# Input scale folded into C, whole-matrix DMA transposes, an idle Pool and searched ranks in a gated S5 and Hedgehog kernel

## The chip, the cores and the metric

The kernel runs on one core of one Trainium2 chip. The metric is the device time of one execution in microseconds (us).

The engines are named as in the profile: PE does matmuls, PEld is PE's loading of weights (it overlaps with matmuls), DVE is the vector engine, ACT the scalar (activation) engine, POOL the GpSimd engine, SP the engine whose queue issues most DMAs. "PEclk" or "granted clock" is the share of full speed at which PE was allowed to run.

## The reference, cut to what matters

The kernel mixes two sequence layers by a gate (S5, a state space layer, and Hedgehog, a linear attention), for S = 2048 positions of D = 512 channels in bf16.

```python
x = A_x
g = _sigmoid((x * gate_w).sum(-1, keepdims=True))

# A: state space part, P = 512 complex states
dt = jnp.exp(log_dt)
Lam_bar = jnp.exp(dt * Lam)
B_bar = ((Lam_bar - 1.0) / Lam)[:, None] * Bmat      # the "input scale" times B
Bu = jnp.einsum("bld,pd->blp", x + 0j, B_bar)
for t in range(L):
    h = Lam_bar[None, :] * h + Bu[:, t, :]
y = 2.0 * jnp.einsum("blp,dp->bld", hseq, Cmat).real + x * Dskip[None, None, :]

# B: linear attention, 32 heads of 16
pq = einsum(q, w_phi); pk = einsum(k, w_phi)
phi_q = concat([softmax(pq), softmax(-pq)]); phi_k = concat([softmax(pk), softmax(-pk)])
kv = einsum(phi_k, v); z = phi_k.sum(s)
o = (phi_q @ kv) / (phi_q @ z + 1e-6)
b = o @ wo

return g * y + (1 - g) * b
```

One identity carries the change. The recurrence is diagonal in the states and linear in its input. So the factor `(Lam_bar - 1) / Lam`, one complex number per state, may be taken out of B and put on the columns of C instead; the states are then unscaled, and y is the same.

## The kernel before: the parts that matter here

**A planner fixes the order.** The kernel does not issue its instructions in the order of its text. Each piece of work is a task: the engines that may do it with an assumed duration in ns for each, what it depends on, the buffers it takes, and a rank (the highest goes first). A list scheduler inside the kernel places the tasks one by one on a model of the engines. What it assumes is therefore built into the order, but nothing of it slows or speeds an instruction.

```python
for t in reversed(self.tasks):
    t.tail = min(t.eng.values()) + min(LAT[e] for e in t.eng) + max([s.tail for s in t.succ], default=0.0)
    t.key = (-t.rank, -t.tail // QUANT, t.n)
while True:
    ...
    t0 = max(f, min(w[0] for w in rs))
    r, took, t = min((w for w in rs if w[0] <= t0 + WINDOW), key=lambda w: w[2].key)
    ...
self.order = sorted(out, key=lambda t: (t.start, t.n))
```

**B is scaled and transposed on PE.** The scale is computed from the parameters by some 17 tiny DVE operations, spread into twelve 128x128 diagonals, and applied by 64 matmuls that transpose B at the same time. Eight evictions from PSUM (the memory into which matmuls accumulate) then write `BT`.

```python
for kk, v in enumerate((b2r, nb2i, nb2r)):                                    # L529
    VS(out=dgB[:, j, kk, :], in0=ident[:], scalar1=v[:, j:j + 1], scalar2=None, op0=ALU.mult)
...
MM(out=f32v(b)[:, cs], lhsT=Bn[:, 0, j, ds_], rhs=dgB[:, j, c0, :], start=True, stop=False)   # L622
MM(out=f32v(b)[:, cs], lhsT=Bn[:, 1, j, ds_], rhs=dgB[:, j, c1, :], start=False, stop=True)
t = pl.add(_pe(8, 128), mm, deps=t_db + [d_b], bufs=[b, early[3]])
t_bt[ri, dt] = evac_task(BT[:, dt, :, :, ri], b, ...)
```

**Pool builds the recurrence diagonals.** `dgL` holds the complex multiplication by `Lam_bar` as a 128x128 matrix for each of eight blocks of states.

```python
nc.gpsimd.tensor_tensor(out=dgL[:], in0=ident..., in1=lr_[:, 4:12]..., op=ALU.mult)    # L549
nc.gpsimd.tensor_tensor(out=dgS[:], in0=swap..., in1=ns1[:, 4:12]..., op=ALU.mult)     # L553
nc.gpsimd.tensor_tensor(out=dgL[:], in0=dgL[:], in1=dgS[:], op=ALU.add)                # L557
```

**The state space matmuls.** Positions are taken as 512 chunks of four. Positions 0 to 2 of all chunks are kept as partial states `Gs`; the fourth position feeds a scan over the chunks on DVE (`scan_unit`), and `fill_unit` adds the scanned state back to the first three.

```python
MM(out=f32v(b), lhsT=BT[:, kt, tt].rearrange("p q r -> p (q r)"), rhs=xT[...], ...)    # L639
MM(out=f32v(b), lhsT=dgL[:, tt, :], rhs=Gs[:, tt, f - 1, :], start=False, stop=True)   # L644
# fourth position: L653 with BT, L658 with half of dgL
```

**The keys' softmax, and Pool once more.** For each of eight pairs of position tiles, `E` is the exponential, and DVE adds it up in a tree to `st1`. Pool adds `st1` into `smax` (only used for a final range flag). ACT then takes the logarithm in place, so it must wait until Pool has read `st1`.

```python
nc.gpsimd.tensor_tensor(out=smax[:], in0=smax[:], in1=b1.t[:]..., op=ALU.add)          # L773
aact(out=b1.t[:], in_=b1.t[:], func=ACT.Ln)               # deps: prev + t_sx[-1:]
aact(out=rc.t[:], in_=b1.t[:], func=ACT.Exp, scale=-1.0)
VT(out=e5(), in0=e5(), in1=rc.t[:]..., op=ALU.mult)       # normalise E, L777
```

**The join.** After the last pair, the key-value sums leave PSUM as `KVbd` and `SM`. Everything of the queries after this needs them. This code is the same before and after.

```python
VT(out=KVbd[qr, sgn].rearrange("p g (d h) -> p g h d", d=Dh)[:, :, half * 4:half * 4 + 4, :],   # L826
   in0=a4[:, :, :, 0:Dh], in1=mask4[pr]..., op=ALU.mult)
VT(out=SM[qr, sgn, :, 1, half * 4:half * 4 + 4], in0=a4[:, :, :, Dh], in1=mask4[pr]..., op=ALU.mult)   # L828
```

## Time and profile before

| what | before |
|---|---|
| time, median (range) | 182.97 us (182.79 to 183.77, 3 runs) |
| span of the profiled run | 182.4 us |
| PE / DVE / ACT / POOL busy | 162.7 / 146.9 / 108.9 / 18.5 us |
| mean granted clock | 0.950 |
| first state space matmul (L639) | 37.8 us after the start |

The page gives the busy time of each engine, the granted clock in 40 slices of the span (in tenths, 9 is 90% or more), and the share of each engine in the chain of work that ended last. Of the page of the kernel before:

```profile
PE 162.7 (89%) x1274; PEld 89.0 (49%) x1293; DVE 146.9 (81%) x369; ACT 108.9 (60%) x217; POOL 18.5 (10%) x27
...
PEclk9999996999999999999966998589999999999998
...
DVE 47%; PE 36%; DMA 5%; issue 4%; ACT 2%; POOL 2%; SPq 1%; DVEq 0%; POOLq 0%; ACTq 0%
```

PE is the busiest engine at 89%, yet the chain runs over DVE more than over PE. The clock dips in three places: in the slice from 27 to 32 us (the first 6), from 91 to 100 us (66) and from 109 to 123 us (858). The table of stretches shows these places; its columns are the stretch, its length, busy time and number of instructions of PE, PEld, DVE, ACT and POOL, the granted clock, the DMA share and GB/s. Of the kernel before:

```profile
core 0: us, PE busy (x) PEld busy (x) DVE busy (x) ACT busy (x) POOL busy (x), PEclk, DMA share, GB/s
...
25.00:30.00 5.00, 2.64 (x24) 2.28 (x24) 4.89 (x18) 4.35 (x8) 0.00 (x0) 0.75 0.46 105
30.00:35.00 5.00, 4.40 (x57) 3.68 (x56) 4.88 (x9) 4.83 (x7) 0.00 (x0) 0.91 0.43 99
...
90.00:95.00 5.00, 3.62 (x83) 2.75 (x85) 5.00 (x8) 3.44 (x8) 0.00 (x0) 0.74 0.01 3
95.00:100.00 5.00, 5.00 (x15) 1.90 (x14) 4.49 (x14) 3.51 (x8) 0.77 (x1) 0.58 0.20 48
...
110.00:115.00 5.00, 2.54 (x72) 2.07 (x71) 4.92 (x9) 0.77 (x2) 0.00 (x0) 0.78 0.01 3
115.00:120.00 5.00, 4.77 (x46) 2.56 (x45) 4.97 (x16) 1.38 (x5) 0.00 (x0) 0.53 0.00 0
```

In all three places PE pauses while DVE is full or nearly so, and the granted clock falls in the pause and in the stretch behind it. From 115 to 120 us PE is busy for 4.77 us, but at 0.53 of full speed.

Why the first state space matmul comes so late can be read in the timeline. Its columns are the start, the duration, the engine, the line, the operation with its tiles, and in brackets the idle time before it and what ended that. First Pool, then DVE in the same stretch, then PE, all of the kernel before:

```profile
15.38 1.92 POOL L549 TENSOR_TENSOR dgL<-ident,sp 128x1024 bf16<-128x1024 bf16 x1 [4.52 <-DVE sp L508]
20.07 1.92 POOL L553 TENSOR_TENSOR dgS<-swap,sp 128x1024 bf16<-128x1024 bf16 x1 [2.76 <-DVE sp L537]
22.06 2.13 POOL L557 TENSOR_TENSOR dgL<-dgL,dgS 128x1024 bf16<-128x1024 bf16 x1
```

```profile
15.38 0.16 DVE L511 TENSOR_TENSOR sp<-v_66 128x12 f32<-128x12 f32 x1
15.58 1.75 DVE L512 TENSOR_TENSOR sp<-sp 128x12 f32<-128x12 f32 x1
17.25 0.16 DVE L513 TENSOR_SCALAR sp<-sp 128x12 f32<-128x12 f32 x1
...
20.14 1.87 DVE L542 TENSOR_TENSOR sp<-sp 128x12 f32<-128x12 f32 x1
...
22.25 1.98 DVE L545 TENSOR_SCALAR sp<-sp,sg 128x12 f32<-128x12 f32 x1
```

```profile
36.05 1.89 PE L434 MATMUL pp<-Wv,xT 128*128 128x512 bf16 x7
37.78 1.46 PE L639 MATMUL pp<-xT,BT 128*128 128x512 bf16 x6
```

Operations on 128x12 elements take 0.16 us, and three of them take 1.75, 1.87 and 1.98 us. Each of the three begins just after a Pool operation begins and ends with it (15.58 + 1.75 = 17.33 against 15.38 + 1.92 = 17.30). The Trainium skill, "SBUF — State Buffer", section "SBUF: two separate sides", says that GpSimd shares a pair of ports, under an exclusive lock, with DVE operations in a two-port mode or with two SBUF inputs: whoever starts first holds it for its whole instruction and the other blocks fully. This trace agrees, with 1.75 to 1.98 us in place of 0.16. The block is about 5 us of DVE time, on the way to everything that depends on the parameters.

The waits view lists, for an engine and line, what it waited for: total us, number of times, longest. Of the kernel before:

```profile
PE pp L605 <- ACT vx L393: 3.4, 1, 3.4
...
ACT st_1150 L248 <- POOL smax L773: 2.9, 1, 2.9
...
PE pp L907 <- DVE SM L828: 2.4, 1, 2.4
...
ACT st_795 L248 <- POOL smax L773: 2.2, 1, 2.2
```

The logarithm of the keys' softmax waits for Pool's `smax` for 9.3 us in six places together (two are shown). The longest of these waits stands before the second dip of the clock: Pool's addition, 0.45 us at its quickest, takes 1.98 us from 86.84 us on, ACT waits for it, DVE's normalisation of `E` (89.88 us) waits 1.4 us for ACT, and PE waits 1.3 us for that `E` until 91.16 us. PE waits for `SM` at the join, before the third dip.

### The profile page before, as it was taken

The numbers are of one execution on the slowest core, as the hardware profiler recorded it, in microseconds if no ns is written. First come the engines' busy times: TensorE is split into PE (matmuls) and PEld (weight loads), VectorE is DVE, ScalarE is ACT, GpSimd is POOL, SyncE is SP. The second block draws the span as 40 slices with busy tenths as digits, with TensorE's granted clock in tenths as the row PEclk, the third lists the DMA queues.
The fourth block names the chain that finished last, engine by engine and source line by source line (L and its number), as shares of the span: only waits on it lengthen the run. The fifth ranks groups of instructions, "written<-read, shape, count | busy, mean of one in ns | idle before, by whom it ended". The sixth has DMA issues, their size and how long they took to land.

```text
span 182.4 us, 3458 instructions
## 1 busy us (share of the span) xinstructions
PE 162.7 (89%) x1274; PEld 89.0 (49%) x1293; DVE 146.9 (81%) x369; ACT 108.9 (60%) x217; POOL 18.5 (10%) x27
## 2 busy tenths in 40 slices
PE   7699929899999998998799994989999999999980
PEld 2465408744444543452363553655565655566530
DVE  4499999955899997999698999999999992574130
ACT  2288639920773965675567990269998745367200
POOL 6134530000002003101401000000000000000000
PEclk9999996999999999999966998589999999999998
DMA  6999454650004003103102200000101000100111
GB/s 202 295 350 141 117 142 91 146 142 0 0 0 103 15 0 84 33 4 74 41 4 58 58 0 0 4 4 2 59 31 61 29 29 32 59 29 32 45 49 36
DMA packets 17983, 11.85 MB, mean 65 GB/s; under 512 B 10280, under 2 KB 17448, under 8 KB 17960
## 3 DMA queue, kind: packets, MB, share of 16 engines
q1 hardware_dynamic: 17392, 11.54, 23.3%
q8 instruction: 12, 0.20, 0.4%
q10 hardware_dynamic: 568, 0.02, 0.2%
q14 instruction: 11, 0.09, 0.2%
HBM read 4.22 MB, written 2.10 MB: 35 GB/s over the span
## 4 chain that ended last, share of the span: by engine, by line
DVE 47%; PE 36%; DMA 5%; issue 4%; ACT 2%; POOL 2%; SPq 1%; DVEq 0%; POOLq 0%; ACTq 0%
PE pp L961 11%; PE pp L639 6%; PE pp L977 5%; DVE c L692 4%; DVE late L953 3%; DMA xn<-in_A_x_dram 3%; DVE KVbd L826 3%; DVE E L777 3%; DVE c L722 2%; DVE c L723 2%; POOL smax L773 2%; PE pp L753 2%; PE pp L653 2%; PE pp L907 2%; DVE late L955 2%
## 5 line engine op out<-in xcount | busy, mean ns | idle before, releaser
L639 PE MATMUL pp<-xT,BT 128*128 128x512 bf16 x95 | 23.4, 379 | 0.1
L961 PE MATMUL pp<-CT,Gs 128*128 128x512 bf16 x91 | 22.9, 379 | 0.3
L248 ACT ACTIVATE ET<-pp 128x512 bf16<-128x512 f32 x32 | 17.1, 648 | 3.2 <-PE pp L842 3.2
L949 ACT CAST late<-pp 128x512 bf16<-128x512 f32 x32 | 17.0, 615 | 3.0 <-PE pp L946 3.0
L842 PE MATMUL pp<-xT,Wq_70 128*128 128x512 bf16 x61 | 17.2, 431 | 0.7 <-ACT late L949 0.4
L248 ACT ACTIVATE E<-pp 128x512 bf16<-128x512 f32 x32 | 16.3, 613 | 0.9 <-PE pp L753 0.4
L985 DVE TENSOR_SCALAR late<-pp,Gg 128x512 bf16<-128x512 f32 x8 | 6.0, 752 | 12.9 <-PE pp L977 12.9
L977 PE MATMUL pp<-Wo,late 128*128 128x512 bf16 x62 | 16.0, 379 | 0.2 <-issue 0.2
L434 PE MATMUL pp<-Wv,xT 128*128 128x512 bf16 x61 | 14.7, 379 | 0.6 <-ACT xT L393 0.3
L953 DVE TENSOR_TENSOR late<-late 128x512 bf16<-128x512 bf16 x32 | 12.8, 428 | 2.6 <-ACT late L949 2.3
L753 PE MATMUL pp<-Wk_71,xT 128*128 128x512 bf16 x61 | 14.7, 379 | 0.2
L639 PEld LDWEIGHTS <-BT 128*128 128x128 bf16 x96 | 9.3, 98 | 11.1
L961 PEld LDWEIGHTS <-Gs 128*128 128x128 bf16 x96 | 8.9, 98 | 8.8
L393 ACT CAST Gs<-pp 128x512 bf16<-128x512 f32 x17 | 9.9, 604 | 5.2 <-PE pp L644 5.1
L777 DVE TENSOR_TENSOR E<-E,rc 128x2048 bf16<-128x2048 bf16 x8 | 9.8, 1220 | 3.5 <-ACT rc L248 3.5
L973 ACT COPY late<-pp 128x512 bf16<-128x512 bf16 x16 | 9.3, 599 | 5.2 <-PE pp L977 3.6
L842 PEld LDWEIGHTS <-Wq_70 128*128 128x128 bf16 x64 | 6.7, 109 | 9.0 <-issue 4.3
L946 PE MATMUL pp<-KVbd,ET 128*128 128x128 bf16 x128 | 9.6, 219 | 0.1
L393 ACT CAST vx<-pp 128x512 bf16<-128x512 f32 x16 | 8.7, 600 | 1.5 <-PE pp L434 1.2
L961 PE MATMUL pp<-CT,Zs 128*128 128x512 bf16 x31 | 9.3, 439 | 0.2 <-issue 0.2
L434 PEld LDWEIGHTS <-xT 128*128 128x128 bf16 x64 | 6.0, 98 | 6.9 <-issue 0.8
L692 DVE TENSOR_TENSOR_SCAN c<-sp,c 128x512 bf16<-128x512 f32 x8 | 9.3, 1207 | 0.0
(250 smaller groups left out, 314.9 us busy)
## 6 DMA issues: line engine op xcount, KB each, us to landing
xn<-in_A_x_dram SPq DMA_DIRECT2D x4, 512.0 KB, 4.3
Zs<-c SPq DMA_DIRECT2D x32, 64.0 KB, 2.0
out_dram<-late SPq DMA_DIRECT2D x16, 128.0 KB, 1.9
CT<-Gs SPq DMA_DIRECT2D x4, 256.0 KB, 3.4
Wv<-in_B_wqkv_dram SPq DMA_DIRECT2D x1, 512.0 KB, 4.3
Bn<-in_A_B_re_dram SPq DMA_DIRECT2D x1, 512.0 KB
Bn<-in_A_B_im_dram SPq DMA_DIRECT2D x1, 512.0 KB
Wo<-in_B_wo_dram SPq DMA_DIRECT2D x4, 128.0 KB, 2.6
```

Of the source, the lines that this page charges most:

```text
L248: return nc.scalar.activation(**kw)
L393: nc.scalar.copy(out=o, in_=view(b))
L434: MM(out=f32v(b), lhsT=xT[:, kt, tcols(f, a)], rhs=Wv[:, kt, :], start=(kt == 0), stop=(kt == KT - 1))
L639: MM(out=f32v(b), lhsT=BT[:, kt, tt].rearrange("p q r -> p (q r)"), rhs=xT[:, kt, f * NCH:(f + 1) * NCH], start=(kt == 0), stop=(kt == KT ...
L692: nc.vector.tensor_tensor_scan(out=bw_.t[:, ri], data0=rb, data1=b1.t[:, ri], initial=0.0, op0=ALU.mult, op1=ALU.add)
L753: MM(out=f32v(b), lhsT=xT[:, kt, tcols(f, a)], rhs=Wk2[:, kt, :], start=(kt == 0), stop=(kt == KT - 1))
L777: x = pl.add(_dve(1024), lambda e: VT(out=e5(), in0=e5(), in1=rc.t[:].to_broadcast([P, 32, Dh, 4]), op=ALU.mult), deps=[x], bufs=[eb, rc], ...
L842: MM(out=f32v(b), lhsT=Wq2[:, kt, g * P:(g + 1) * P], rhs=xT[:, kt, f * NCH:(f + 1) * NCH], start=(kt == 0), stop=(kt == KT - 1))
L949: tn = pl.add(_act(512), lambda e, sgn=sgn: nc.scalar.copy(out=o2.t[:, sgn], in_=f32v(pn[sgn])), deps=[t], bufs=[pn[sgn], o2], rank=rank + 2)
L953: VT(out=v, in0=v, in1=als[f].t[:, a, sgn * H:(sgn + 1) * H].rearrange("p (g h) -> p g h", g=HG).unsqueeze(2).to_broadcast([P, HG, Dh, 8]) ...
L961: MM(out=f32v(py), lhsT=st, rhs=CT[:, tt, :], start=(tt == 0), stop=False)
L977: MM(out=f32v(py), lhsT=oT.t[:, g, :], rhs=Wo[:, g, :], start=False, stop=(g == HG - 1))
```

## The change

Its intent: B no longer depends on the parameters, so the state space matmuls can begin as soon as a DMA has transposed B; Pool does nothing in SBUF beside DVE's work on the parameters and the softmax; and the order is better fitted. The core of the diff, long cuts marked:

```diff
+UNIT_RANKS = (
+    -3.39, 2.47, -0.13, 1.09, -2.01, 6.16, 9.56, 18.87, 1.24, ...          # 81 shifts
+def shift(self, by):
+    for t in self.tasks:
+        t.rank += by[t.u] if t.u < len(by) else 0.0
 ...
-    nc.sync.dma_start(out=Bn[:, 0], in_=A_B_re.rearrange("(j p) d -> p j d", p=P))
-    nc.sync.dma_start(out=Bn[:, 1], in_=A_B_im.rearrange("(j p) d -> p j d", p=P))
-    for W_, c0 in ((WkT, D), (WqT, 0)):
-        for j in range(KT):
-            nc.sync.dma_start_transpose(out=W_[:, j, :], in_=B_wqkv[:, c0 + j * P:c0 + (j + 1) * P])
+    for ri, B_ in enumerate((A_B_re, A_B_im)):
+        nc.sync.dma_start_transpose(out=BT[:, :, ri, :], in_=B_)
+    nc.sync.dma_start_transpose(out=WkT, in_=B_wqkv[:, D:2 * D])
+    nc.sync.dma_start_transpose(out=WqT, in_=B_wqkv[:, 0:D])
 ...
-    def b_prep():                         # 64 matmuls against dgB, 8 evictions to BT: all gone
 ...
+    # C: two whole-matrix transposes into cb, then the scale: 8 ACT and 8 DVE operations of 128x512
+    nc.scalar.mul(out=tC[:, ri, :], in_=cb.t[:, 1 - ri, j, :], mul=nb2i[:, j:j + 1])
+    nc.vector.scalar_tensor_tensor(out=o, in0=o, scalar=c0[:, j:j + 1], in1=tC[:, ri, :], op0=ALU.mult, op1=ALU.add)
 ...
-    x1 = pl.add({"POOL": 2400.0}, dl1, ...)          # dgL, dgS, their sum, and Dd on Pool
+    pl.add({"ACT": 210.0, "DVE": 165.0}, scaled(dgL[:, tt, :], ident[:], lr_[:, ucol(tt)]), ...)
+    pl.add({"ACT": 210.0, "DVE": 165.0}, scaled(dgS[:, tt, :], swap[:], ns1[:, ucol(tt)]), ...)
+    # sums by DVE; dgX: copies of dgL spread so that the fourth position's matmuls are full width
 ...
-        MM(out=f32v(b), lhsT=BT[:, kt, tt].rearrange("p q r -> p (q r)"), ...)
+        MM(out=f32v(b), lhsT=BT[:, kt].rearrange("p r (q t) -> p (r q) t", t=NT)[:, :, j + 4 * h], ...)
-        MM(out=f32v(b)[h * 64:h * 64 + 64, :], lhsT=dgL[:, 2 * j + h]..., ...)
+        MM(out=f32v(b), lhsT=dgX[:, j, h, ri, :], ...)
 ...
-        nc.gpsimd.tensor_tensor(out=smax[:], in0=smax[:], in1=b1.t[:]..., op=ALU.add)
-        aact(out=b1.t[:], in_=b1.t[:], func=ACT.Ln)      # deps=prev + t_sx[-1:]
+        nc.vector.tensor_reduce(out=smax[:, pair:pair + 1], in_=b1.t[:]..., axis=AX.X, op=ALU.max)   # rank=-3
+        aact(out=lnk.t[:], in_=b1.t[:], func=ACT.Ln)     # deps=prev
 ...
-            cost.update(_dve(256 if bf else 512))
+            cost.update({"DVE": 375.0 if bf else 640.0})
+    pl.shift(UNIT_RANKS)
```

The weights that a state space matmul reads from `BT` are now every eighth element of a row (every fourth at the fourth position), because B arrives transposed as a whole and is not regrouped on the way.

## The prediction

> **What bounds it now.** PE is busy 162.7 of 182.4 us, DVE 146.9, ACT 108.9 (page). From start-to-start times in the timeline (128x512 matmuls 215 ns, 128x128 56 ns) all matmuls need an estimated 149 us at full clock. First transpose 5.0 us, end 5.4 us after PE's last matmul: the floor of this program is about 159 us, so some 23 us are stalls, in three places.
>
> 1. Before the first state-space matmul at 37.8 us (timeline). PE idles 3.4 us before the Wk fold and runs at clock 0.75 and 0.91 in 25-35 us (windows). The chain of waits is DVE: parameters, tables, dgB, eight 0.7 us BT evictions, with b_prep (64 matmuls, 3.6 us) between. Three tiny 128x12 DVE operations take 1.75-1.98 us instead of 0.17, each ending with a Pool operation on dgL or dgS (15.4-17.3, 20.1-22.0, 22.1-24.2 us). The Trainium skill, "SBUF — State Buffer" (shared port pair), says either engine can block the other for a whole instruction; the coinciding ends agree.
> 2. 40-113 us: DVE nearly full, chain DVE/PE. In-place Ln waits for Pool's smax: ACT waits 9.3 us on it in total (waits view); Pool's 0.45 us operation stretches to 1.7-2.0 us twice, on the chain.
> 3. 85-120 us: PE pauses, clock 0.53-0.78. After 150 us the chain is PE.
>
> **Change.** Removed: 64 b_prep matmuls (-3.6 us PE), eight BT evictions (5.8 us, mostly DVE), twelve dgB scalings (2.1 us), Pool's dgL/dgS/Dd/smax with about 5 us of DVE blocking and the smax waits. Added: DVE/ACT take dgL, dgS, Dd, dgX (about 28 operations, 0.17-0.4 us, estimate 6 us), C scaling (8 DVE operations of about 0.7 us, 8 on ACT of 0.6 us), eight max reductions (2.2 us). DVE about -4 us net. The last g3 matmuls become full width: in before, 16 half-width ones cost about 2.5 us because pairs overlap; now 16 x 0.215, +1 us PE. BT weight loads become strided by 8; stride-2 ones took 98 ns like contiguous ones, so I expect no cost.
> Moved: B now gates PE only through its DMA. A 128-column transpose costs 1.26-2.4 us of SP queue; with two B matrices after x, I expect B at about 21 us, Wk at 27, Wq at 32. x transposes and V (18 us PE) fill until then. The first state-space matmul moves from 37.8 to about 22-24 us.
>
> **Sum.** Floor 159 - 3.6 + 1 = 156.5 us. Stalls: stage 1 gives about 9 us, of which some comes back as DVE waits in the middle (DVE still needs some 140 us); middle and joints give 1-3 us; tail unchanged. Net expected -11.5 us: **171.5 us, 80% range 165.5 to 177.5.** Chances: faster 0.95, same 0.04, slower 0.01.
>
> **Would show it right:** timeline: first state-space matmul at 20-26 us; PE clock 1.0 through 20-40 us; no microsecond-long 128x16 DVE operations; Pool idle after about 4 us; no ACT wait on smax; BT weight loads 98 ns; PE total 159-161 us; PE full after about 145 us; chain in the middle still mixed DVE/PE.
>
> **What would make it wrong:** whole-matrix transposes slower on the queue than four chunks, B or Wk landing after 30 us; parameters (now behind x and weights in the SP queue) delaying dgL and tables, so PE starves on recurrences; ACT overloaded before 40 us by scalings plus table loads; offline order fitted to wrong durations (its plan puts 128x512 fills at 268 ns, the trace has 363), so engines stall; C late.

## The result, and the profile after

| what | before | after |
|---|---|---|
| time, median (range) | 183.02 us (182.79 to 183.77, 4 runs) | 168.44 us (168.17 to 169.15, 4 runs) |
| ratio, 95% interval | | 0.9203 (0.9164 to 0.9242): faster |
| span of the profiled run | 182.4 us | 166.7 us |
| PE / DVE / ACT / POOL busy | 162.7 / 146.9 / 108.9 / 18.5 us | 154.2 / 141.8 / 118.0 / 4.6 us |
| mean granted clock | 0.950 | 0.979 |
| first state space matmul | 37.8 us | 21.9 us |

A ratio is the mean time of one kernel's fast runs over the mean of the other's in the same rounds, so it is not quite the ratio of the medians that stand beside it. Where I give a difference between two kernels that were each timed against the kernel before, I subtract their ratios and multiply by 183.0 us; with the intervals found, such a difference is good to about 1 us. The three groups of runs were on different chips (9, 7 and 2 in the record), each beside the kernel before, so this also takes the ratios to be the same on each chip.

Of the page of the kernel after:

```profile
PE 154.2 (92%) x1231; PEld 89.2 (54%) x1231; DVE 141.8 (85%) x377; ACT 118.0 (71%) x240; POOL 4.6 (3%) x12
...
PEclk9999999999999999999999879999999999999995
...
PE 47%; DVE 34%; ACT 7%; DMA 6%; issue 1%; ACTq 1%; SPq 0%; DVEq 0%
```

The dips of the clock at 27 to 32 us and at 91 to 100 us are gone (the 8 and the 7 that are left in the middle, at 92 to 100 us, belong to the join), and the chain now runs over PE first. The same stretches, and those of the join, which now comes at 88 to 93 us, in the kernel after:

```profile
25.00:30.00 5.00, 4.43 (x21) 2.42 (x20) 4.79 (x22) 5.00 (x11) 0.00 (x0) 1.00 1.00 198
30.00:35.00 5.00, 5.00 (x36) 3.29 (x35) 4.41 (x9) 4.97 (x9) 0.00 (x0) 1.00 0.00 0
...
90.00:95.00 5.00, 2.22 (x38) 1.55 (x39) 4.92 (x12) 1.78 (x6) 0.00 (x0) 0.98 0.22 73
95.00:100.00 5.00, 5.00 (x48) 2.44 (x46) 4.97 (x16) 3.91 (x10) 0.00 (x0) 0.68 0.01 2
```

The early stall is gone. The pause at the join is still there, with the low clock behind it. In the timeline of the kernel after, PE reaches the state space matmuls straight from the values (L448) and the gate (L903), and the tiny DVE operations on the parameters take 0.17 and 0.23 us (L525 is one that Pool blocks again in two experiments below, where it stands on L526). First PE, then DVE:

```profile
17.68 2.75 PE L448 MATMUL pp<-Wv,xT 128*128 128x512 bf16 x12
20.27 1.74 PE L903 MATMUL pp<-gw_b,xT 128*128 128x1 bf16 x64
21.87 3.44 PE L679 MATMUL pp<-xT,BT 128*128 128x512 bf16 x15
```

```profile
20.82 0.17 DVE L525 TENSOR_TENSOR sp<-sp 128x16 f32<-128x16 f32 x1
20.90 0.23 DVE L526 TENSOR_SCALAR sp<-sp,sg 128x16 f32<-128x16 f32 x1
```

In the waits view no operation waits for Pool's `smax` any more. Pool still meets DVE once, at the very start: while it clears `dgX` and `KVbd` until 4.96 us, three copies of 64x64 and 128x64 elements by DVE take 1.27 to 1.40 us, and DVE's first eviction starts at 5.93 us instead of 5.66. The wait for `SM` at the join has not shrunk: it was 2.4 us and is now

```profile
PE pp L954 <- DVE SM L872: 3.1, 2, 2.3
```

The span fell by 15.7 us. By the page, 8.5 us of that is PE busy time and the other 7.2 us is PE idle time. The busy time fell by far more than the removed matmuls. They were 64 of 56 ns from start to start, so 3.6 us, and the full-width matmuls of the fourth position took 1.6 us back (4.1 against 2.5 us busy in the groups view). The rest is mostly the clock: 162.7 us at 0.950 lose an estimated 8.1 us to the clock, 154.2 us at 0.979 lose 3.2 us. That is 4.9 + 3.6 - 1.6 = 6.9 of the 8.5 us. The profiled execution of the kernel before was a slow one within its fast state, 184.15 us at 0.950, where its other runs show 0.948 to 0.970, so the spans differ by more than the medians (14.6 us) and the clock's share is at the high end.

### The profile page after: what moved, and what is told of

It is laid out like the page before. It is cut to its first block, busy times and chain, and to the rows that moved or that the text cites. A ratio compares the mean times of both kernels' runs of the same rounds, so it can differ in the third digit from the quotient of the medians.

```text
span 166.7 us, 3342 instructions
## 1 busy us (share of the span) xinstructions
PE 154.2 (92%) x1231; PEld 89.2 (54%) x1231; DVE 141.8 (85%) x377; ACT 118.0 (71%) x240; POOL 4.6 (3%) x12
## 4 chain that ended last, share of the span: by engine, by line
PE 47%; DVE 34%; ACT 7%; DMA 6%; issue 1%; ACTq 1%; SPq 0%; DVEq 0%
PE pp L1009 17%; PE pp L1025 8%; PE pp L887 5%; DVE c L733 4%; PE pp L994 4%; DVE E L821 4%; DMA vq<-in_A_Lambda_im_dram 4%; DVE ET L607 3%; DVE KVbd L870 3%; PE pp L679 3%; PE pp L1012 2%; ACT E L267 2%; DMA vec_n<-in_gate_w_dram 2%; PE pp L1019 2%; PE pp L954 2%; DVE c L737 1%
## 5 line engine op out<-in xcount | busy, mean ns | idle before, releaser
L1009 PE MATMUL pp<-CT,Gs 128*128 128x512 bf16 x96 | 23.8, 379 | 0.1
L267 ACT ACTIVATE E<-pp 128x512 bf16<-128x512 f32 x32 | 16.6, 632 | 2.3 <-PE pp L828 1.6
L679 PEld LDWEIGHTS <-BT 128*128 128x128 bf16 x96 | 13.6, 145 | 8.0 <-issue 1.4
L887 PE MATMUL pp<-xT,Wq_71 128*128 128x512 bf16 x64 | 16.2, 402 | 0.0
L448 PE MATMUL pp<-Wv,xT 128*128 128x512 bf16 x64 | 14.8, 379 | 0.0
L405 ACT CAST Gs<-pp 128x512 bf16<-128x512 f32 x22 | 12.4, 592 | 1.1 <-PE pp L684 0.6
L405 ACT CAST vx<-pp 128x512 bf16<-128x512 f32 x16 | 9.3, 592 | 2.4 <-PE pp L448 2.2
L797 PEld LDWEIGHTS <-xT 128*128 128x128 bf16 x64 | 6.2, 98 | 7.4 <-issue 0.3
L887 PEld LDWEIGHTS <-Wq_71 128*128 128x128 bf16 x64 | 6.1, 101 | 6.8 <-issue 1.1
L448 PEld LDWEIGHTS <-xT 128*128 128x128 bf16 x64 | 6.1, 98 | 6.6
```

The lines of the kernel that those rows point to most:

```text
L267: return nc.scalar.activation(**kw)
L405: nc.scalar.copy(out=o, in_=view(b))
L448: MM(out=f32v(b), lhsT=xT[:, kt, tcols(f, a)], rhs=Wv[:, kt, :], start=(kt == 0), stop=(kt == KT - 1))
L679: MM(out=f32v(b), lhsT=BT[:, kt].rearrange("p r (q t) -> p (r q) t", t=NT)[:, :, j + 4 * h], rhs=xT[:, kt, f * NCH:(f + 1) * NCH], start=( ...
L797: MM(out=f32v(b), lhsT=xT[:, kt, tcols(f, a)], rhs=Wk2[:, kt, :], start=(kt == 0), stop=(kt == KT - 1))
L887: MM(out=f32v(b), lhsT=Wq2[:, kt, g * P:(g + 1) * P], rhs=xT[:, kt, f * NCH:(f + 1) * NCH], start=(kt == 0), stop=(kt == KT - 1))
```

## The experiments

Three things were done at once: the detour of B over PE went, Pool was taken out, and the order was searched anew. My theory after reading the result was that the first two make the gain and that the search only fits the order to them. The rivals were that the search is the gain, or that only one of the first two is. All twelve kernels gave the reference's result except the one that is wrong. In this section "the planned end" is the end that the kernel's own planner puts on its order. It is no time of the chip, but it is useful to see which of two orders fits its tasks better.

### Taking parts away without refitting the order

**e1_no_ranks.** The shifts are not applied.

```diff
-    pl.shift(UNIT_RANKS)
     pl.run()
```

> The changed kernel with the 81 searched unit ranks not applied (the hand-given ranks inside the units stay), so all of the new algebra, DMA and Pool changes with an unsearched order. Theory (most of the gain is work and waits that are gone before the first state-space matmul, the search fills joints): 171 to 175 us, i.e. the search is worth 3 to 7 us of the 14.6; the first state-space matmul still before 28 us. Rival (the search is what made the gain): 179 us or more.

Measured: 191.47 us, ratio 1.0478 (1.0404 to 1.0551). It is slower than the kernel before, and my theory missed by 16 us or more. The rival's line (179 us or more) was passed, but a result slower than the kernel before is more than the loss of a gain. In its waits view:

```profile
PEld L828 <- DVE E L821: 18.9, 5, 13.3
PE pp L828 <- DVE E L821: 17.7, 3, 12.8
ACT lnk L267 <- DVE st L814: 12.4, 3, 9.6
```

PE stands for 12.8 us at a stretch for a normalised `E` that DVE was told to make late; the mean clock is 0.909. The planned end rises from 156.5 to 178.1 us, so the planner itself sees that its hand-set ranks don't suit the changed program. What follows is a warning about the method: a program whose ranks were fitted with everything in place cannot be judged by taking the ranks away. The 23 us are not the worth of the search; they are the price of an unfit order (what an order alone gives is measured below, by e12). The next two kernels carry the same flaw.

**e2_bprep_back.** B again loaded plainly and transposed on PE: 64 matmuls against diagonals of ones and zeros that are made from the parameters (so the dependence is there again), eight evictions. The scale stays in C.

```diff
-        nc.sync.dma_start_transpose(out=BT[:, :, ri, :], in_=B_)
+        nc.sync.dma_start(out=Bn[:, :, ri, :], in_=B_.rearrange("(j p) d -> p j d", p=P))
+        ... # 12 scalings to dgB from (1, 0, 1); 64 matmuls; 8 evictions to BT
-        bt_all = [d_b]
+        bt_all = t_bt
```

> The changed kernel with B prepared by PE again: B loaded untransposed, 64 matmuls against diagonals that depend on the parameters (ones and zeros, so the result stays right), eight evictions, twelve scalings; ranks and the scaled C stay. Theory (the detour through parameters, diagonals and evictions held the first state-space matmul back): plus 5 to 9 us, first state-space matmul at 28 to 33 us. Rival (only the engine work counts): plus 3.6 us of PE or less.

Measured: 179.13 us, ratio 0.9804 (0.9774 to 0.9835).

**e4_pool_back.** `dgL`, `dgS`, `Dd` and `smax` back on Pool, planned anew with the old shifts.

```diff
-    parts.append(pl.add({"ACT": 210.0, "DVE": 165.0}, scaled(dgL[:, tt, :], ...)))   # and dgS, Dd
+    x1 = pl.add({"POOL": 2400.0}, lambda e: diag(dgL, ident, lr_), deps=[tp3], rank=6)   # and dgS, the sum, Dd
-    nc.vector.tensor_reduce(out=smax[:, pair:pair + 1], ..., op=ALU.max)
+    nc.gpsimd.tensor_tensor(out=smax[:], in0=smax[:], in1=b1.t[:]..., op=ALU.add)    # Ln in place again
```

> The changed kernel with dgL, dgS, Dd and the running smax on Pool again, Ln in place behind smax, all else as changed. Theory (Pool and DVE block each other, ACT waits for smax): DVE operations of 1.5 us or more on 128x16 or 128x512 tiles reappear beside Pool's, smax operations stretch to 1 to 2 us, total plus 2 to 5 us. Rival (Pool was off the critical path and takes work from DVE and ACT): no slower than the changed kernel.

Measured: 183.23 us, ratio 1.0011 (0.9986 to 1.0036). The whole gain is gone, although the first state space matmul starts at 24.6 us. But the planned ends rose too (167.7 for e2, 162.5 for e4), so neither number separates the part from the order. Both lost more than I had expected, 11.0 us (e2) and 14.8 us (e4) against the kernel after, and had to be repeated.

**e5_contig_w.** The weights are read contiguously from `BT`, so the wrong rows of B are used. Its output is wrong, which doesn't matter for the time.

```diff
-    lhsT=BT[:, kt].rearrange("p r (q t) -> p (r q) t", t=NT)[:, :, j + 4 * h]
+    lhsT=BT[:, kt, h, j * P:(j + 1) * P]
```

> The changed kernel with the BT weight loads reading 128 contiguous columns instead of every 8th or 4th (the wrong columns, so the result is wrong on purpose; program, order and waits are the same). Theory (loads of 144 ns still hide under a 215 ns matmul): loads fall to 98 ns, time within 0.5 us of the changed kernel. Rival (the 47 ns of 96 loads are paid): 3 to 5 us faster.

Measured: 168.02 us, ratio 0.9204 (0.9174 to 0.9234), the same as the kernel after. In the groups view (busy us, then mean ns of one), the loads of the kernel before, of the kernel after and of e5 in this order:

```profile
L639 PEld LDWEIGHTS <-BT 128*128 128x128 bf16 x96 | 9.3, 98 | 11.1
```

```profile
L679 PEld LDWEIGHTS <-BT 128*128 128x128 bf16 x96 | 13.6, 145 | 8.0 <-issue 1.4
```

```profile
L679 PEld LDWEIGHTS <-BT 128*128 128x128 bf16 x96 | 9.2, 97 | 11.7 <-issue 1.5
```

Weights at a step of eight elements load in 145 ns instead of 97. Nothing of that reaches the time, because a load runs beside the matmul before it: a 128x512 matmul follows the last one by 216 ns in either kernel. The Trainium skill, "TensorE: Matmul & The Clock Gate", section "Weight-path perf modes — Fast Weight Load (FWL) and DoubleRow", allows the fast load for strided columns. It doesn't say that a wide step is slower, which these traces show.

### One cause at a time, in the order of the kernel after

These four leave the planner's tasks as they are, so the order is the same (compared instruction by instruction) and only the operations differ.

**e4f_pool_fixed.** Pool does `dgL`, `dgS`, `Dd` and `smax` in the slots of the planned order.

```diff
-    scaled(dgL[:, tt, :], ident[:], lr_[:, ucol(tt)])
+    lambda e, tt=tt: diag(dgL, ident, lr_) if tt == 0 else None          # and dgS, the sum, Dd
-    nc.vector.tensor_reduce(out=smax[:, pair:pair + 1], ...)
+    # in the slot of Ln: Pool's add into smax, then Ln in place
```

> dgL, dgS, Dd and smax on Pool again (Ln in place behind smax), but with the order on PE, DVE, ACT and the DMA queue kept exactly as in the changed kernel; the run with Pool back and a newly planned order lost all 14.8 us, and its order was no longer the searched one. Theory (Pool itself costs through blocked DVE operations and ACT waiting for smax): plus 2 to 6 us, tiny DVE operations of 1.5 us or more beside Pool's. Rival (the 14.8 us came from ranks that no longer fit the tasks): plus less than 2 us.

Measured: 176.63 us, ratio 0.9635 (0.9592 to 0.9678), so 7.9 us more than the kernel after and more than I expected. In its timeline a 128x16 operation takes 1.89 us beside a Pool operation again. In its waits view the new waits are

```profile
ACT dgX L589 <- POOL dgL L582: 6.2, 1, 6.2
ACT st L267 <- POOL smax L824: 6.2, 6, 2.1
DVE dgX L591 <- POOL dgL L582: 4.2, 1, 4.2
```

The first and the third are latency: Pool's three operations run one after the other until 28.0 us, later than the order counted on. So all three ways in which Pool's work can cost time are seen in this run (blocking DVE, coming late, holding up the logarithm). How much of the 7.9 us each costs was not separated, and the sum overstates what a fitted order would pay.

**e6_pe_plus** and **e7_dve_plus.** Is the kernel after bound by PE or by DVE? One adds a matmul of zeros to each of 16 key tiles, 16 x 0.216 = 3.45 us of PE. The other does eight products of the scan's rotation twice, about 5 us of DVE.

```diff
+    if kt == 0:                                                           # e6
+        MM(out=f32v(b), lhsT=xT[:, kt, tcols(f, a)], rhs=warm[:], start=False, stop=False)
+    VT(out=b1.t[:], in0=bw_.t[:], in1=c2, op=ALU.mult)                    # e7, in r1 and in r4
```

> The changed kernel with one more 128x512 matmul (of zeros, the result stays right) in each of the 16 k tiles, 3.45 us of PE work between 35 and 85 us, order unchanged. Theory (PE binds once the stalls are out): plus 3 to 4 us. Rival (DVE binds in that stage and PE has slack): plus under 1.5 us.

> The changed kernel with two of the 0.69 us rotations of each of the four scans issued twice, 5 us of DVE work (0.6 us start to start each) between 35 and 90 us, order unchanged, result right. If PE alone binds: plus under 2 us. If DVE binds there: plus 4 to 5.5 us. I expect 3 to 5, because DVE is full in every 5 us window from 40 to 130.

Measured: e6 172.23 us, ratio 0.9423 (0.9379 to 0.9466), so 4.0 us for 3.45 us added. e7 174.52 us, ratio 0.9533 (0.9480 to 0.9586, one of four runs slow and left out), so 6.0 us for about 5 us added, above the 3 to 5 us that I had expected. Both engines pass on all that they are given, so neither has room for more work in that stage; by the chain view they take turns there. It doesn't follow that a saving on either engine counts in full, since the other may still bind after it. The only saving that was measured is the next run, at a place where PE waits for DVE.

**e8_kv_order.** The join's evictions write `KVbd` in runs of four neighbouring elements instead of one element every 16 bytes. The price is that they read PSUM at a step of 17 elements instead of contiguously.

```diff
-    VT(out=KVbd[qr, sgn].rearrange("p g (d h) -> p g h d", d=Dh)[:, :, half * 4:half * 4 + 4, :], in0=a4[:, :, :, 0:Dh],
-       in1=mask4[pr].unsqueeze(1).unsqueeze(3).to_broadcast([64, HG, 4, Dh]), op=ALU.mult)
+    VT(out=KVbd[qr, sgn].rearrange("p g (d h) -> p g d h", d=Dh)[:, :, :, half * 4:half * 4 + 4], in0=a4[:, :, :, 0:Dh].rearrange("p g h d -> p g d h"),
+       in1=mask4[pr].unsqueeze(1).unsqueeze(1).to_broadcast([64, HG, Dh, 4]), op=ALU.mult)
```

> The changed kernel with the four KVbd evictions written in the order in which KVbd lies (head innermost) and not by 16-byte steps; order and result unchanged. They take 1.29 us each for 64x256, 5.2 us in a row at 88 to 93 us, while PE waits 3.1 us for SM behind them and its clock falls to 0.68. If the write order is what makes them slow: 0.4 to 0.6 us each and 2 to 4 us off the total. Rival (the slowness is the PSUM read or the mask): 1.29 us still, no gain.

Measured: 165.03 us, ratio 0.9027 (0.8982 to 0.9072), so 3.2 us less than the kernel after. In the groups view, the kernel after and then e8:

```profile
L870 DVE TENSOR_TENSOR KVbd<-pp,mask_88 64x256 bf16<-64x256 f32 x4 | 5.2, 1290 | 0.1
```

```profile
L870 DVE TENSOR_TENSOR KVbd<-pp,mask 64x256 bf16<-64x256 f32 x4 | 1.7, 421 | 0.1
```

The same product of 64x256 elements takes 421 ns instead of 1290 ns; PE's wait for `SM` is gone, and the mean clock rises from 0.979 to 0.997. The Trainium skill, "SBUF — State Buffer", section "Specifications (TRN2)", says that SBUF has lines of 16 bytes and needs two hits in a line for full bandwidth. One bf16 element every 16 bytes has one hit per line. That fits, but the edit changes the order of the write, of the read and of the mask together, so the write's step is the likely cause and not a shown one. The planner had counted 423 ns for a whole `KVbd` and `SM` pair, where the trace shows 1.32 us from pair to pair. So the search had no reason to prepare for this stall. This is the pause at the join, which both kernels have.

### Parts again, each with an order that suits it

For the last four, the ranks were searched for each program by itself: simulated annealing over the unit shifts, with the planned end as the goal.

**e12_before_search.** The kernel before, with nothing but such shifts added. Planned end 160.8 to 157.1 us.

```diff
+    pl.shift(UNIT_RANKS)      # searched for the kernel before; units named as in the change
     pl.run()
```

> The kernel before, with nothing changed but the order: units marked as in the changed kernel and their ranks searched by me (two annealing searches of 200 and 240 s over the kernel's own planner). The planner's own end time: before 160.8 us, this 157.1, changed kernel 156.5; the trace ends 21.6 us after the planner for before, 10.2 us after it for the changed kernel. Theory (what the planner does not know, Pool blocking DVE and the like, stays in this program): 178 to 181 us. Rival (a searched order is what the changed kernel gained by): under 172 us.

Measured: 178.90 us, ratio 0.9748 (0.9681 to 0.9814; the verdict at 2% is unclear). The order alone is worth 4.6 us on the kernel before. ACT still waits 10.2 us on `smax`, and the first state space matmul still starts only at 33.9 us.

**e2s_bprep_search.** e2 with searched ranks (planned end 160.5 us).

```diff
-UNIT_RANKS = ( ... )          # of the kernel after
+UNIT_RANKS = ( ... )          # searched for e2
```

> B prepared by PE again as in the earlier run of that change (179.1 us with ranks that did not fit), now with ranks searched for it in the same way. Planner's end 160.5 us against 156.5 of the changed kernel. Theory (the detour through parameters and PE costs 4 to 5 us when the order is right; the rest of the 10.7 us was misfit ranks): 171 to 174 us. Rival (the detour itself costs the 10.7 us): 177 us or more.

Measured: 172.55 us, ratio 0.9423 (0.9373 to 0.9472), so 4.0 us more than the kernel after. The planned ends differ by the same 4.0 us. The first state space matmul moved back by 10.5 us, to 32.4 us, but only 4.0 us arrive at the end: with a fitted order, PE does other work first. Of the page of e2s:

```profile
PE 157.4 (92%) x1273; PEld 92.6 (54%) x1295; DVE 145.1 (85%) x389; ACT 122.6 (72%) x250; POOL 4.6 (3%) x12
```

In its span of 170.4 us PE is idle for 13.0 us, against 12.5 us in the kernel after. So the 4.0 us are about the PE work of the 64 matmuls (3.6 us from start to start; e6 paid 4.0 us for 3.45 us of PE work), and PE's later start on the state space matmuls costs next to nothing beyond it, within the error of 1 us. This is what the rival of e2 said (only the engine work counts), and not my theory.

**e4s_pool_search.** e4 with searched ranks (planned end 155.1 us).

```diff
-UNIT_RANKS = ( ... )          # of the kernel after
+UNIT_RANKS = ( ... )          # searched for e4
```

> dgL, dgS, Dd and smax on Pool again, with ranks searched for that program. The planner, which knows nothing of Pool and DVE blocking each other, ends at 155.1 us, 1.4 us before the changed kernel. Theory (Pool costs what the planner does not see): 172 us or more, with blocked DVE operations in the trace. Rival (Pool's chain costs only when the order doesn't allow for its latency): 169 us or less.

Measured: 173.92 us, ratio 0.9485 (0.9433 to 0.9538), so 5.2 us more than the kernel after. The planner had promised 1.4 us less. In its timeline, with Pool's operations beside the blocked DVE ones:

```profile
18.68 2.91 POOL L575 TENSOR_TENSOR dgL<-ident,sp 128x1024 bf16<-128x1024 bf16 x1 [3.00 <-DVE sp L522]
22.05 1.91 POOL L575 TENSOR_TENSOR dgS<-swap,sp 128x1024 bf16<-128x1024 bf16 x1 [0.46 <-DVE sp L529]
24.04 2.12 POOL L579 TENSOR_TENSOR dgL<-dgL,dgS 128x1024 bf16<-128x1024 bf16 x1
```

```profile
19.73 1.88 DVE L526 TENSOR_TENSOR sp<-sp 128x16 f32<-128x16 f32 x1
...
22.17 1.83 DVE L535 TENSOR_TENSOR sp<-sp 128x16 f32<-128x16 f32 x1
...
24.20 2.00 DVE L538 TENSOR_TENSOR sp<-sp,vp 128x16 f32<-128x16 f32 x1
```

The three blocked operations take 5.2 us more than three of 0.17 us. No planner with a duration for each task can see this, because it happens only when two tasks meet. ACT also waits 5.1 us for `smax` again. Which of the two makes how much of the 5.2 us was not separated by a run: none has only `smax` on Pool. The trace points to the blocked operations and the late diagonals. From 20 to 40 us PE is busy for 15.70 us at a clock of 0.91, where the kernel after has 19.43 us at 1.00; over the whole span PE is idle for 16.6 us against 12.5 us, so nearly all of the difference is in that stretch, and Pool's first addition to `smax` comes later, at 47.42 us. In that stretch the chain runs through the three blocked operations to an eviction by DVE, for which PE waits:

```profile
PE pp L689 <- DVE Gs L408: 4.2, 1, 4.2
```

**e13_kv_search.** e8's eviction order, and the ranks searched further with it (planned end 153.8 us).

```diff
 # KVbd written as in e8, and:
-UNIT_RANKS = ( ... )          # of the kernel after
+UNIT_RANKS = ( ... )          # searched further
```

> The changed kernel with the four KVbd evictions in storage order (165.0 us in the earlier run) and with ranks searched further (planner's end 153.8 us instead of 156.5). If the planner is now a fair model (trace end 5.7 us after it in that run): 161.5 to 163.5 us, faster than both kernels. If it is exhausted: 165 us or more.

Measured: 161.87 us (161.01 to 162.28, 6 runs), ratio 0.8813 (0.8777 to 0.8848). This beats both kernels. Of its page:

```profile
PE 151.7 (95%) x1210; PEld 89.4 (56%) x1231; DVE 137.9 (86%) x376; ACT 118.1 (74%) x241; POOL 4.5 (3%) x12
...
PEclk9999999999999999999999999999999999999999
```

With no pause left that the clock answers to, the same matmuls as in the kernel after are 151.7 us of busy time in place of 154.2 us, in a span of 160.1 us.

### The account

| part (the first two undone alone, the third added to the kernel before; all with a searched order) | worth |
|---|---|
| B's detour over PE (e2s against after), nearly all of it the work of its 64 matmuls | 4.0 us |
| Pool's work on SBUF (e4s against after) | 5.2 us |
| the searched order (e12 against before) | 4.6 us |
| sum, against 14.6 us measured | 13.8 us |

So my theory held in part; its reason for the detour's worth, the late first state space matmul, did not hold. The two program changes make about two thirds of the gain, and the search makes about a third where it can be measured cleanly. The rivals that name one cause alone fall. The sum comes out close, but that parts add up was not shown: the order's worth was measured on the other kernel than the two parts, and each has an error of about 1 us. Not measured alone: the cost of the C scaling (5.7 us of DVE and 5.5 us of ACT in the groups view), the full-width fourth position, and whole-matrix transposes against four chunks each.

## Why the prediction was right, point by point

The time was predicted as 171.5 us (165.5 to 177.5) and came out at 168.44 us; "faster" was right. The point estimate was 3.1 us high.

- **The first stage: right in its course.** I predicted the first state space matmul at 22 to 24 us; it is at 21.9 us. The clock is 1.00 from 20 to 40 us, as predicted. B landed at about 17 us and not at 21, because a whole-matrix transpose of B takes 1.9 us of the SP queue and lands 5.0 to 5.9 us after its issue; four chunks at my 1.26 to 2.4 us each were too pessimistic. What this earlier start is worth is the next point.
- **"Stage 1 gives about 9 us": too much; the term lumps two causes.** Measured with a fitted order, the detour alone gives 4.0 us (e2s), although it moves the first matmul by 10.5 us, and the 64 matmuls, which I had already taken off the floor as 3.6 us, make nearly all of that. PE's wait for B is then worth next to nothing. Pool's part, which I had put at about 5 us of blocking, costs 5.2 us together with the `smax` waits (e4s).
- **Pool: right.** No DVE operation on 128x16 elements takes a microsecond any more, Pool is idle after about 5 us, and no wait on `smax` is left.
- **The mis-sized term: "middle and joints give 1-3 us".** I gave the new order no value of its own; the only word about the offline search was a risk. On the kernel before, a searched order alone gives 4.6 us (e12). So the total came near in part by luck: the wait for B was valued too high and the order at nothing, and the two errors lean against each other. No run splits the order's worth by stage, and so none says where the missing 3.1 us lie.
- **"PE total 159-161 us": wrong, 154.2 us.** I took the busy time of before, subtracted the removed matmuls and added the new ones. Busy time is not work: 8.1 us of the old figure was the low clock (an estimate from 162.7 us at 0.950), and that shrank when the pauses did. e13, at a clock of 1.00, has 151.7 us.
- **"BT weight loads 98 ns": wrong, 145 ns; "I expect no cost": right.** I went from a step of two to a step of eight without any measurement in between. e5 shows that the 47 ns are hidden.
- **"The chain in the middle still mixed DVE/PE": right.** e6 and e7 show it more sharply than the chain does: both engines pass on every added microsecond.
- **"PE full after about 145 us": too cautious.** PE is full from about 95 us, right after the join.
- **The fear of an order fitted to wrong durations: right in kind, wrong in place.** I had named the fills. The trace shows a wrong duration that stalls PE at the join, where the planner counts 423 ns and a pair takes 1.32 us. Its evictions start 20.3 us earlier than before (87.71 against 107.96 us), but the span is only 15.7 us shorter: what comes from the join on takes 4.6 us longer than before (why was not tested). Mending the eviction gave 3.2 us (e8).

## What to carry to other kernels

A tiny DVE operation that takes microseconds, and that ends together with a Pool operation, is blocked and not slow; take Pool off SBUF there, and price that by the whole instruction that it holds up. Don't judge a part of a program whose order was fitted to the whole by removing the part alone: refit the order first, or keep it fixed, and say which (the detour of B seemed to cost 11 us with the wrong order and 4.0 us with a fitting one). And when pauses go, PE's busy time falls too, since the clock falls in and behind pauses; predict from start-to-start times at full clock and not from the busy time.

## What the Trainium skill lacked or had wrong

- "TensorE: Matmul & The Clock Gate", "Weight-path perf modes — Fast Weight Load (FWL) and DoubleRow": it lacks the cost of a step within the fast load. 128x128 bf16 weights took 98 ns at steps of one and two elements, 113 ns at four and 145 ns at eight.
- The same page, "Back-to-back issue gap": it gives about 131 ns per matmul of 512 columns as the sustained rate in a stream of loads and matmuls, and 216 ns as the isolated gap, which it says over-counts. Here such a stream, each matmul with its own load, ran at 216 ns (12 matmuls in 2.75 us, the last of them recorded as 0.38 us), so the formula held and the lower figure did not.
- "SBUF — State Buffer", "Specifications (TRN2)": it asks for two hits in a line of 16 bytes for full bandwidth and gives no size for what fewer cost. A DVE product of 64x256 elements that writes one bf16 every 16 bytes took 1290 ns, and 421 ns when it writes runs of four; the experiment changed the order of the read and of the mask as well, so the 869 ns between them are not shown to be the write's alone.
- "DMA: Bandwidth & Descriptors", "DMA Transpose (X-bar)": it gives no duration of a transpose; elsewhere the page has an effective bandwidth, and sequencer cycles for small tiles, but no time for a whole matrix from issue to landing. Four 512x512 bf16 matrices (B and C) took 1.9 to 2.5 us of the queue and landed 4.6 to 5.9 us after their issue; 512 columns cut from a matrix 1536 wide took 3.5 to 3.9 us of the queue, and one of the two landed after 8.1 us.
